# A planner's lengths and transfer model, the rank of its row maxima, and tail scores in four quadrants

## The chip, the cores and the metric

The kernel runs on one core of one Trainium2 chip. The metric is device time in microseconds (us), lower is better: the median of the runs. The engines are PE (TensorE, matmuls; its weight loads are PEld), DVE (VectorE), ACT (ScalarE), POOL (GpSimd) and SP (SyncE, which here only issues DMAs). Each engine takes its instructions in the order in which the program gives them.

## The reference

Attention over 4 batches, 8 heads, 576 positions, 64 features, then two mixture layers on the 512 joined features:

```python
q_rot, k_rot = (rotate(q), rotate(k))
scores = scale * np.matmul(q_rot, k_rot.transpose(0, 1, 3, 2))
scores = scores - np.max(scores, axis=-1, keepdims=True)
attn = np.exp(scores); attn = attn / (np.sum(attn, axis=-1, keepdims=True) + 1e-09)
x = np.matmul(attn, v)
# first mixture layer; x_prev is x one position earlier
xk = mu_k * x + (1.0 - mu_k) * x_prev
xr = mu_r * x + (1.0 - mu_r) * x_prev
k = np.maximum(xk @ w_k, 0.0); v = k * k @ w_v
x = 1.0 / (1.0 + np.exp(-(xr @ w_r))) * v
# second mixture layer
h = np.maximum(x @ w_in, 0.0); u, v = (h[..., :512], h[..., 512:])
v_n = (v - mean(v)) / np.sqrt(var(v) + 1e-06)
out = (u * (np.einsum('ts,bsd->btd', w_spatial, v_n) + b_spatial[None, :, None])) @ w_out
```

## The kernel before, in words

**The parts.** Attention of all four batches is interleaved with the first mixture layer's two large products (w_k, w_v). Both are cut into steps, and a planner written in Python puts the steps into an order for each engine. Behind it come the rest of the first layer (w_r and the gate) and the second layer, in an order written out by hand (line 785 on). Their tiles take the place of attention's, so their weight loads start once attention is over.

**Units.** Two heads make a pair, four pairs a batch. A pair's 576 rows of queries are four blocks of 128 and a tail of 64. A batch has 18 units (`which`, line 297): eight blocks of pairs 0 to 3 (units 0 to 7, first two blocks of each), two tail units (8 and 9, each with the last 64 rows of two pairs), eight more blocks. 72 units in all, eight of them tails. A unit goes through these steps, one line of the plan each (lines 538 to 558):

- `scores` (L318, PE): two PSUM tiles `s`; for a block, head j of the pair in tile j, contraction over 64 rows of the array; each tile has 288 columns in each of two halves, so 4 calls of matmul. For a tail, pair u has tile u, its two heads on the upper and lower 64 partitions: 8 calls. There are only two `s` tiles, so a unit's scores wait for the exponentials of the unit before. A call appears in the trace as two matmuls.
- `top` (L324, DVE, twice): the negated maximum of each row. `expo` (L329, ACT, twice): the exponential with its sum. `norm` (L334, L335, DVE). `high` (L341, ACT, twice) and `low` (L345, DVE, twice): the scaled probabilities as two f16 parts, into `p16`.
- `turn` (L350): SP issues one DMA that transposes `p16` into `pt`, of which there are three.
- `values` (L370, PE): 36 matmuls of 128x64 (72 for a tail), which read `pt` and `vv`; `gather` (L380 to L388, ACT) copies to `xt`, and POOL stores it (L397, L399).

**What comes ahead of a pair.** SP loads q and k (L218, L220) into one of two `raw` buffers; `rope` on DVE (L225, L226) rotates them into `rot` and so frees `raw`. v is loaded (L230), its maximum taken (L234), spread over the partitions by POOL (L238), split (L253, L258) and copied on SP (L263, L264).

**First mixture layer** (`moe1`, line 476), twice a batch, of 256 and 320 positions: `mix` (L415 to L422), dots with w_k (L432, PE) and with w_v (L462, PE), squares between them (L441 to L450), the result stored by SP (L474). The weights w_k and w_v come in 16 loads (L157) at the start, each joined from two words on ACT and DVE (L162 to L174).

**The planner** (`Plan`, line 39). Each step has a rank (about the unit in which it is due), an engine, a length in us, the steps and the buffers that it needs. `order` (line 55) runs a clock: whenever an engine is free it takes, of its next 80 steps by rank, the first whose needs are done and whose buffers are free. The program is then given out in that order, and on the chip each engine follows it, whatever the true lengths are. A step with `dma` adds to one queue of transfers (lines 81 to 83): it lands when all transfers ahead of it have had their lengths. `HOP`, 0.15, is added to each end.

Of the kernel before, what the change touches and what calls it, by code (L numbers as in the profile page):

```python
# [7 lines left out]
F32 = mybir.dt.float32  # L8
# [14 lines left out]
HALF = S // 2  # L23
# [15 lines left out]
class Plan:  # L39
# [15 lines left out]
    def order(self):  # L55
# [4 lines left out]
        while any(todo.values()):  # L60
# [7 lines left out]
            for engine, xs in todo.items():  # L68
                if free.get(engine, 0.) > now:
                    continue  # L70
                for k, x in enumerate(xs[:80]):
                    rank, _, _, us, fn, name, needs, take, use, dma = x
                    t = max([done.get(n, 1e9) for n in needs], default=0.)
                    tags = [tag for tag, _ in take]
                    if t > now:
                        soon.append(t)
                    elif all(self.room[tag] >= tags.count(tag) for tag in tags):
                        for tag in tags:
                            self.room[tag] -= 1
                        end = free[engine] = now + us  # L80
                        if dma:
                            queue = max(queue, end + 1.2) + dma
                            end = queue + .5
                        done[name] = end + self.HOP
                        back.append((end + self.HOP, [b for _, b in take] + list(use)))
                        out.append((now, x))
                        del xs[k]
                        break
# [8 lines left out]
def body(ctx: ExitStack, tc, qp, kp, vp, cs, mu_k, mu_r, w_k, w_v, w_r, w_in, w_sp, b_sp, w_out, out):  # L97
# [111 lines left out]
    def prep(i, s):  # L209
# [61 lines left out]
        for w in range(2):  # L271
# [7 lines left out]
            else:  # L279
                add(r - 2, "SP", .1, lambda w=w: load(1 - w, 0), ("ld", i, 1 - w), needs=pace(r - 2),  # L280
                    take=[("raw", ("raw", i, 1 - w))], dma=2.2)
                needs = [("ld", i, 1 - w)]
            add(r, "DVE", 2.2, lambda w=w: rope(1 - w), ("rope", i, 1 - w), needs=needs, use=[("raw", i, 1 - w)],
                take=[("rot", ("rot", i, 1 - w))])
        add(s - 5, "SP", .1, v_load, ("vl", i), needs=pace(s - 5), take=[("vr", ("vr", i))], dma=1.2)
        add(s - 3.5, "DVE", .8, v_max, ("vmax", i), needs=[("vl", i)], use=[("vr", i)], take=[("vm", ("vm", i))])
# [4 lines left out]
        add(s - .4, "DVE", .89, v_low, ("vlow", i), needs=[("v5", i)], use=[("vm", i), ("vr", i)])  # L291
        add(s - .3, "SP", .2, v_copy, ("vcopy", i), needs=[("vlow", i)], use=[("vv", i)], dma=.4)

# [13 lines left out]
    def scores(m):  # L307
        ps = [ps_s.tile([128, 2, 512], F32, tag="s", name=f"s{n}")
              for n in (2 * m, 2 * m + 1)]
        w = which(m)  # L310
        for u in range(2 if w[0][2] == 64 else 1):
            i, c, n, _ = w[u]
            q, k = preps[i][0], preps[i][1]
            for h in range(2):
                for j in range(2):
                    r = HEAD[j]
                    o = ps[u][r, h, :HALF] if n == 64 else ps[j][:, h, :HALF]
                    nc.tensor.matmul(o, q[r, c:c + n], k[r, h * HALF:(h + 1) * HALF], start=True, stop=True)  # L318
        sm = at.tile([128, 4, 2], F32, tag="sm", bufs=4, name=f"sm{m}")
        units[m] = [[x[:, :, :HALF] for x in ps], sm, [None, None], None]  # L320
# [35 lines left out]
    def values(m):  # L356
# [6 lines left out]
        for us in ((0,), (1,)) if w in (8, 9) else ((0, 1),):  # L363
            for kc in range(NKC):
                for hl in range(2):
                    for j in range(2):
                        u = us[j % len(us)]
                        i, _, n, o = which(m)[u]
                        a = pt[:, u, kc, HEAD[j]] if n == 64 else pt[:, u, kc, :]
                        nc.tensor.matmul(pv[HEAD[j], o:o + n], preps[i]["vv"][:, kc, j, D * hl:D * hl + D], a,  # L370
# [65 lines left out]
    def k_square(b, h, fc):  # L436
        ps = mo.pop((b, h, "k", fc))[:, :PART[h][1]]
        if fc % 2 == 0:
            mo[b, h, "s"] = moe_tile([128, 2, PART[1][1]], F32, "rl", 2, name=f"rl{b}_{h}_{fc}")[:, :, :PART[h][1]]
        rl = k2 = mo[b, h, "s"]  # L440
        nc.scalar.activation(rl[:, fc % 2, :], ps, AF.Relu)  # L441
# [34 lines left out]
    def moe1(b, h):  # L476

        end = UN * b + (20 if h else 10)
        s, places = end + 1.6, 16 if h else 20
        at_ = lambda m: s + .5 * (m * places / 16)  # L480
# [17 lines left out]
        for fc in range(NFC):  # L498
            m = at_(fc)
            bank, q, r = ("m", P, fc), fc // 2, ("rl", P, fc // 2)  # L500
            for k in range(2):
                add(m + .1 * k, "PE", .9 * f, lambda fc=fc, k=k: k_dot(b, h, fc, k), ("k", P, fc, k),
                    needs=[("x3", P, 2 * k), ("x3", P, 2 * k + 1)] + [("wlo", c + 4 * (fc // 4)) for c in (2 * k, 2 * k + 1)]
# [11 lines left out]
        for dc, half in ((0, 0), (1, 0), (0, 1), (1, 1), (2, 0), (2, 1), (3, 0), (3, 1)):  # L515
            m = at_(8 + n)
            n += 1
            for k in (2 * half, 2 * half + 1):
                add(m + .1 * (k % 2), "PE", .9 * f, lambda dc=dc, k=k: v_dot(b, h, dc, k), ("v", P, dc, k),
                    needs=[("kl", P, k), ("wlo", 8 + 2 * k), ("wlo", 9 + 2 * k)] + ([("v", P, dc, k - 1)] if k else []),  # L520
                    take=[] if k else [("m", ("mv", P, dc))], use=[("kk", P, k)] + ([("mv", P, dc)] if k else []))
            if half:
                add(m + .6, "ACT", .39 * f, lambda dc=dc: v_out(b, h, dc), ("vo", P, dc), needs=[("v", P, dc, 3)],
                    use=[("mv", P, dc)], take=[("mf", ("vs", P, dc))])
                add(m + 1, "SP", .1, lambda dc=dc: v_store(b, h, dc), ("vst", P, dc), needs=[("vo", P, dc)],
                    use=[("vs", P, dc)], dma=.6)
# [7 lines left out]
    for m in range(N):  # L534
        b, w = divmod(m, UN)
        pairs = sorted({u[0] for u in which(m)})
        rots = [(i, a) for i in pairs for a in range(2)]
        add(m - .5, "PE", 1.17, lambda m=m: scores(m), ("s", m), needs=[("rope", *r) for r in rots] + [("s", m - 1)][:m],
            use=[("rot", *r) for r in rots], take=[("s", ("s", m, 0)), ("s", ("s", m, 1)), ("sm", ("sm", m))])
        for j in range(2):  # L540
            add(m - .4 + .01 * j, "DVE", .71, lambda m=m, j=j: top(m, j), ("top", m, j), needs=[("s", m)], use=[("s", m, j)])
            add(m - .3 + .01 * j, "ACT", .93, lambda m=m, j=j: expo(m, j), ("exp", m, j), needs=[("top", m, j)],
# [6 lines left out]
        add(m, "DVE", .37, lambda m=m: norm(m), ("norm", m), needs=[("exp", m, 0), ("exp", m, 1)], use=[("sm", m)])  # L549
        add(m + .7, "SP", .1, lambda m=m: turn(m), ("turn", m),  # L550
            needs=[("low", m, 0), ("low", m, 1)] + [("turn", m - 1)][:m], use=[("p16", m)],
            take=[("pt", ("pt", m))], dma=3.4)
        first = w in (0, 4, 8, 10, 14)
        if first:
            bank = ("pvb", m)
        add(m + 1.5, "PE", 1.15, lambda m=m: values(m), ("pv", m),
            needs=[("turn", m)] + [("vcopy", i) for i in pairs] + ([("pv", m - 1)] if m else []),
            use=[("pt", m)] + [("vv", i) for i in pairs] + ([] if first else [bank]), take=[("pvb", bank)] if first else [])
        if w in (3, 7, 9, 13, 17):
# [5 lines left out]
            for i in mine:  # L565
# [3 lines left out]
                if w != 9:  # L569
                    add(m + 2.5, "POOL", .7, lambda i=i, h=int(w > 9): x_store(i, h), ("xst", i, w > 9),  # L570
                        needs=[("xt", m), ("edge", i)] + ([("xt", UN * b + 9)] if w > 9 else []),
                        use=[("xt", i, int(w > 9))], dma=1.2)

# [6 lines left out]
    for c in range(16):  # L580
# [6 lines left out]
        ww, wg = ("ww", c), ("wg", c)  # L587
        add(c - 2, "SP", .1, fns[0], ("wl", c), needs=pace(c - 2), take=[("kk", ww)], dma=2.)
        add(c + .2, "ACT", 1.4, fns[1], ("wsc", c), needs=[("wl", c)], use=[ww], take=[("wg", wg)])
# [264 lines left out]
```

## Time and profile before

| what | before |
|---|---|
| median of 3 runs | 818.85 us (816.68 to 818.96) |
| the profiled execution | 818.47 us, span 816.7 us |
| PE busy | 716.5 us (88%), PEld 622.7 (76%) |
| DVE busy | 548.4 us (67%) |
| ACT busy | 487.0 us (60%) |
| POOL busy | 107.8 us (13%) |
| mean granted clock of PE | 0.941 |
| DMA queue of SP (q1) | 195794 packets, 107.79 MB, 58.0% of 16 engines' span |

The span is the time from the first to the last instruction of the profiled execution; the time of a run is a little longer. Busy shares are means over parts with different limits, so a change is judged in the stretch where it lies. The profile's chain is followed back from the last instruction to whatever released it; its waits name who ended an engine's idle time. The granted clock is the share of PE's full 2.4 GHz; 0.5 is the lower level, 1.2 GHz.

### The profile page before, as it was taken

The page shows a single profiled execution, that of the slowest core. Times are in us where ns is not written, and L with a number is a line of the kernel's source. Part 1 is how long each engine was busy: PE and PEld are TensorE (multiplying, and loading weights), DVE is VectorE, ACT ScalarE, POOL GpSimd, SP SyncE. Part 2 cuts the span into 40 slices and gives each one's busy share as a digit, 9 for nine tenths or more (in the row PEclk, how much of TensorE's full clock was granted, in tenths as well). Part 3 has the DMA queues.
Part 4 walks back from the last instruction along what each step waited for, and adds up shares of the span by engine and source line. Part 5 has one row for each costly group of instructions (what it writes and reads, how often), then busy time and mean ns, then how long its engine had stood idle before and what let it go on. Part 6 is the DMA issues. An engine that isn't in the chain of part 4 may idle for free.

```text
span 816.7 us, 16914 instructions
## 1 busy us (share of the span) xinstructions
PE 716.5 (88%) x6872; PEld 622.7 (76%) x6872; DVE 548.4 (67%) x935; ACT 487.0 (60%) x980; POOL 107.8 (13%) x171
## 2 busy tenths in 40 slices
PE   2267698779999689998899997978899999999997
PEld 1144477558888568897688887977899999998997
DVE  4997999877589887689975664768756232635211
ACT  2657877569678488577695886876633412523311
POOL 0214312111001010001110001351301000201000
PEclk9975889969999889999799999998999999999999
DMA  7879987888589967699986767567210302010101
GB/s 252 248 174 192 248 198 133 201 175 147 148 192 210 209 129 160 134 210 218 180 140 126 127 126 191 164 202 243 59 59 1 117 8 96 29 31 1 59 1 59
DMA packets 197552, 114.19 MB, mean 140 GB/s; under 512 B 172961, under 2 KB 177057, under 8 KB 197474
## 3 DMA queue, kind: packets, MB, share of 16 engines
q1 hardware_dynamic: 195794, 107.79, 58.0%
q0 software_dynamic: 1536, 4.73, 1.8%
q8 instruction: 54, 0.88, 0.4%
q10 hardware_dynamic: 144, 0.59, 0.2%
q14 instruction: 24, 0.20, 0.1%
HBM read 52.26 MB, written 14.16 MB: 81 GB/s over the span
## 4 chain that ended last, share of the span: by engine, by line
PE 50%; DVE 4%; ACT 4%; DMA 4%; issue 1%; POOL 0%; DVEq 0%; ACTq 0%; SPq 0%
PE sp L625 7%; PE mv L462 6%; PE mk L432 6%; PE o L625 6%; PE s L318 5%; PE hv L699 5%; PE r L625 5%; PE u L625 5%; PE pv L370 4%; DMA pt<-p 1%; DMA I-8206_8207<-w_sp 1%; DMA I-8247_8248<-w_out 1%; DMA I-7579_7580<-w_in 1%; DMA I-7623_7624<-w_in 1%; DVE sm L324 1%
## 5 line engine op out<-in xcount | busy, mean ns | idle before, releaser
L318 PE MATMUL s<-rot,rot 64*128 64x288 f32 (+1 forms) x640 | 129.1, 481 | 55.6 <-ACT pf L329 41.9
L329 ACT ACTIVATE pf<-s,sm 128x576 f32<-128x576 f32 x144 | 106.2, 739 | 58.7 <-DVE sm L324 57.9
L318 PEld LDWEIGHTS s<-rot,rot 64*128 64x128 f32 (+1 forms) x640 | 66.9, 199 | 91.9 <-ACT pf L329 55.9
L432 PE MATMUL mk<-x,wk 128*128 128x256 f32 (+1 forms) x768 | 121.0, 307 | 12.0 <-ACT x L420 7.1
L341 ACT ACTIVATE p<-pf,sm 128x576 f16<-128x576 f32 x144 | 109.4, 771 | 36.6 <-DVE sm L335 17.5
L324 DVE TENSOR_REDUCE sm<-s 128x1 f32<-128x576 f32 x144 | 107.0, 751 | 34.9 <-PE s L318 34.6
L345 DVE SCALAR_TENSOR_TENSOR p<-pf,sm,p 128x576 f16<-128x576 f32 x144 | 118.9, 833 | 17.2 <-ACT p L341 17.1
L432 PEld LDWEIGHTS mk<-x,wk 128*128 128x128 f32 x768 | 107.3, 193 | 25.0 <-ACT x L420 7.9
L462 PE MATMUL mv<-kk,wv 128*128 128x256 f32 (+1 forms) x768 | 117.9, 302 | 1.5 <-DVE kk L450 1.5
L370 PEld LDWEIGHTS <-vv 128*64 128x64 f16 x2880 | 89.1, 122 | 36.6 <-issue 30.0
L462 PEld LDWEIGHTS mv<-kk,wv 128*128 128x128 f32 x768 | 104.8, 189 | 14.1 <-issue 10.3
L370 PE MATMUL pv<-pt,vv 128*64 128x128 f16 (+1 forms) x2880 | 100.1, 232 | 17.0 <-DMA pt<-p 16.9
L625 PE MATMUL r<-xr,wr 128*128 128x288 f32 x384 | 55.6, 302 | 2.7 <-DVE xr L629 2.1
L625 PEld LDWEIGHTS r<-xr,wr 128*128 128x128 f32 x384 | 53.6, 194 | 3.8 <-DVE xr L629 2.6
L699 PE MATMUL hv<-wi,x 128*128 128x512 f32 x192 | 48.7, 402 | 6.9 <-ACT x L628 6.7
L625 PE MATMUL sp<-ws,vn 128*128 128x288 f32 x384 | 53.9, 295 | 0.0
L625 PE MATMUL u<-x,wi 128*128 128x288 f32 x384 | 53.6, 298 | 0.0
L625 PEld LDWEIGHTS u<-x,wi 128*128 128x128 f32 x384 | 52.8, 190 | 1.0
L625 PE MATMUL o<-g,wo 128*128 128x288 f32 x384 | 53.0, 296 | 0.5 <-ACT os L755 0.5
L625 PEld LDWEIGHTS sp<-ws,vn 128*128 128x128 f32 x384 | 52.4, 188 | 0.7
L625 PEld LDWEIGHTS o<-g,wo 128*128 128x128 f32 x384 | 51.7, 188 | 1.4 <-ACT os L755 1.2
L699 PEld LDWEIGHTS hv<-wi,x 128*128 128x128 f32 x192 | 35.9, 192 | 14.7 <-ACT x L628 6.9
(293 smaller groups left out, 836.6 us busy)
## 6 DMA issues: line engine op xcount, KB each, us to landing
raw<-kp SPq DMA_DIRECT2D x15, 576.0 KB, 4.7
raw<-qp SPq DMA_DIRECT2D x15, 576.0 KB, 4.5
vr<-vp SPq DMA_DIRECT2D x16, 320.0 KB, 3.8
v<-vd SPq DMA_DIRECT2D x16, 288.0 KB, 2.9
out<-os SPq DMA_DIRECT2D x16, 288.0 KB, 2.1
vv<-vv SPq DMA_DIRECT2D x32, 128.0 KB, 3.2
x<-xd SPq DMA_DIRECT2D x12, 288.5 KB, 3.2
xd<-xt POOLq DMA_DIRECT2D x16, 160.0 KB, 4.5
```

Source lines behind the costliest of these rows:

```text
L318: nc.tensor.matmul(o, q[r, c:c + n], k[r, h * HALF:(h + 1) * HALF], start=True, stop=True)
L324: nc.vector.tensor_reduce(sm[:, 0, j:j + 1], ps[j], axis=AX.XY, op=ALU.max, negate=True)
L329: nc.scalar.activation(pf[j].rearrange("p (a b) -> p a b", a=2), ps[j], AF.Exp, bias=sm[:, 0, j:j + 1], scale=1.0, accum_out=sm[:, 1, j:j ...
L341: nc.scalar.mul(p16[:, j, 0, :], pf[j], sm[:, 3, j:j + 1])
L345: nc.vector.scalar_tensor_tensor(p16[:, j, 1, :], pf[j], sm[:, 3, j:j + 1], p16[:, j, 0, :], op0=ALU.mult, op1=ALU.subtract)
L370: nc.tensor.matmul(pv[HEAD[j], o:o + n], preps[i]["vv"][:, kc, j, D * hl:D * hl + D], a, start=kc + hl == 0, stop=kc + hl == NKC)
L432: nc.tensor.matmul(ps[:, :PART[h][1]], wk[c][fc // 4][:, w, fc % 4 * 128:fc % 4 * 128 + 128], a[:, c, :], start=m == 0, stop=m == 11)
L462: nc.tensor.matmul(ps[:, :PART[h][1]], wv[fc][:, w, dc * 128:(dc + 1) * 128], a, start=m == 0, stop=m == 23)
L625: nc.tensor.matmul(ps[:, h, :HALF], w, a[:, h * HALF:(h + 1) * HALF], start=m == 0, stop=m == n - 1)
L699: nc.tensor.matmul(ps[:, :FS], x[a][:, d, c:c + 128], wi[w][:, d, FS:], start=k == 0, stop=k == 11)
```

## The change

It changes lengths of steps in the plan and how the plan models transfers; gives the row maxima a rank one slot lower; starts the first mixture layer's dots 0.4 of a slot later; computes a tail's scores with the second pair on the other two quadrants of the array, calls alternating between pairs, and lets `values` read the halves so; and keeps the squares' tile under a key of its own for each two blocks. The cut diff:

```diff
@@ Plan.order
                         if dma:
-                            queue = max(queue, end + 1.2) + dma
-                            end = queue + .5
+                            queue = max(queue, now + 1.2) + dma
+                            end = max(queue, end + 1.5) + .4
@@ prep: loads of q and k, of v, copy of v
-                add(r - 2, "SP", .1, lambda w=w: load(1 - w, 0), ("ld", i, 1 - w), needs=pace(r - 2),
-                    take=[("raw", ("raw", i, 1 - w))], dma=2.2)
+                add(r - 2, "SP", .4, lambda w=w: load(1 - w, 0), ("ld", i, 1 - w), needs=pace(r - 2),
+                    take=[("raw", ("raw", i, 1 - w))], dma=1.9)
-        add(s - 5, "SP", .1, v_load, ("vl", i), needs=pace(s - 5), take=[("vr", ("vr", i))], dma=1.2)
+        add(s - 5, "SP", .4, v_load, ("vl", i), needs=pace(s - 5), take=[("vr", ("vr", i))], dma=1.05)
-        add(s - .3, "SP", .2, v_copy, ("vcopy", i), needs=[("vlow", i)], use=[("vv", i)], dma=.4)
+        add(s - .3, "SP", 1., v_copy, ("vcopy", i), needs=[("vlow", i)], use=[("vv", i)], dma=.5)
@@ scores
-        for u in range(2 if w[0][2] == 64 else 1):
-            i, c, n, _ = w[u]
-            q, k = preps[i][0], preps[i][1]
-            for h in range(2):
+        for h in range(2):
+            for u in range(2 if w[0][2] == 64 else 1):
+                i, c, n, _ = w[u]
+                q, k = preps[i][0], preps[i][1]
                 for j in range(2):
                     r = HEAD[j]
-                    o = ps[u][r, h, :HALF] if n == 64 else ps[j][:, h, :HALF]
+                    o = ps[u][HEAD[j ^ u], h, :HALF] if n == 64 else ps[j][:, h, :HALF]
                     nc.tensor.matmul(o, q[r, c:c + n], k[r, h * HALF:(h + 1) * HALF], start=True, stop=True)
@@ values
-                        a = pt[:, u, kc, HEAD[j]] if n == 64 else pt[:, u, kc, :]
+                        a = pt[:, u, kc, HEAD[j ^ u]] if n == 64 else pt[:, u, kc, :]
@@ k_square
-            mo[b, h, "s"] = moe_tile(
...
-        rl = k2 = mo[b, h, "s"]
+            mo[b, h, "s", fc // 2] = moe_tile(
...
+        rl = k2 = mo[b, h, "s", fc // 2]
@@ moe1
-        s, places = end + 1.6, 16 if h else 20
+        s, places = end + 2, 16 if h else 20
-                add(m + .1 * k, "PE", .9 * f, lambda fc=fc, k=k: k_dot(b, h, fc, k), ("k", P, fc, k),
+                add(m + .1 * k, "PE", .94 * f, lambda fc=fc, k=k: k_dot(b, h, fc, k), ("k", P, fc, k),
-                add(m + .1 * (k % 2), "PE", .9 * f, lambda dc=dc, k=k: v_dot(b, h, dc, k), ("v", P, dc, k),
+                add(m + .1 * (k % 2), "PE", .94 * f, lambda dc=dc, k=k: v_dot(b, h, dc, k), ("v", P, dc, k),
-                add(m + 1, "SP", .1, lambda dc=dc: v_store(b, h, dc), ("vst", P, dc), needs=[("vo", P, dc)],
+                add(m + 1, "SP", .4, lambda dc=dc: v_store(b, h, dc), ("vst", P, dc), needs=[("vo", P, dc)],
@@ units
-        add(m - .5, "PE", 1.17, lambda m=m: scores(m), ("s", m), needs=[("rope", *r) for r in rots] + [("s", m - 1)][:m],
+        add(m - .5, "PE", 1.24, lambda m=m: scores(m), ("s", m), needs=[("rope", *r) for r in rots] + [("s", m - 1)][:m],
-            add(m - .4 + .01 * j, "DVE", .71, lambda m=m, j=j: top(m, j), ("top", m, j), needs=[("s", m)], use=[("s", m, j)])
+            add(m - 1.4 + .01 * j, "DVE", .71, lambda m=m, j=j: top(m, j), ("top", m, j), needs=[("s", m)], use=[("s", m, j)])
-        add(m + .7, "SP", .1, lambda m=m: turn(m), ("turn", m),
+        add(m + .7, "SP", 2.8, lambda m=m: turn(m), ("turn", m),
             needs=[("low", m, 0), ("low", m, 1)] + [("turn", m - 1)][:m], use=[("p16", m)],
-            take=[("pt", ("pt", m))], dma=3.4)
+            take=[("pt", ("pt", m))], dma=1.7)
-        add(m + 1.5, "PE", 1.15, lambda m=m: values(m), ("pv", m),
+        add(m + 1.5, "PE", 1.2, lambda m=m: values(m), ("pv", m),
@@ stores of x, weight loads
-                    add(m + 2.5, "POOL", .7, lambda i=i, h=int(w > 9): x_store(i, h), ("xst", i, w > 9),
+                    add(m + 2.5, "POOL", .6, lambda i=i, h=int(w > 9): x_store(i, h), ("xst", i, w > 9),
-                        use=[("xt", i, int(w > 9))], dma=1.2)
+                        use=[("xt", i, int(w > 9))], dma=.6)
-        add(c - 2, "SP", .1, fns[0], ("wl", c), needs=pace(c - 2), take=[("kk", ww)], dma=2.)
+        add(c - 2, "SP", .5, fns[0], ("wl", c), needs=pace(c - 2), take=[("kk", ww)], dma=1.8)
```

## Rows read from the trace of the kernel before

**Rows 1.** Stretch, length; PE, PEld, DVE, ACT, POOL busy us (instructions); PEclk, DMA share, GB/s.

```profile
13.00:150.00 137.00, 95.56 (x973) 68.92 (x974) 125.13 (x199) 97.96 (x202) 34.33 (x38) 0.85 0.89 210
150.00:183.00 33.00, 22.29 (x213) 17.25 (x212) 26.70 (x49) 17.39 (x37) 3.36 (x7) 0.74 0.83 173
183.00:262.00 79.00, 79.00 (x983) 66.84 (x983) 60.44 (x107) 59.91 (x133) 6.17 (x17) 1.00 0.78 169
262.00:295.00 33.00, 23.61 (x263) 18.69 (x262) 27.26 (x50) 20.18 (x43) 3.31 (x6) 0.79 0.86 187
295.00:380.00 85.00, 85.00 (x1023) 71.89 (x1023) 66.96 (x119) 63.36 (x141) 7.51 (x19) 1.00 0.85 168
380.00:410.00 30.00, 25.12 (x266) 18.50 (x264) 26.45 (x51) 20.63 (x45) 3.51 (x5) 0.83 1.04 203
410.00:496.00 86.00, 85.30 (x1092) 73.31 (x1090) 58.17 (x107) 65.82 (x146) 5.77 (x16) 1.00 0.72 131
496.00:583.00 87.00, 71.99 (x508) 67.68 (x507) 62.66 (x91) 64.72 (x116) 30.29 (x29) 0.94 0.61 185
```

**Rows 2.** The chain that ended last, in order of time: start, length (us), what.

```profile
317.86 2.09 PE s L318 x16
...
332.98 1.17 PE s L318 x8
...
336.12 1.13 PE pv L370 x36
...
338.32 1.17 PE s L318 x8
...
496.12 4.59 DMA pt<-p
```

**Rows 3.** Waits (us, times, longest): start twice, then the three gaps in turn.

```profile
PE s L318 <- ACT pf L329: 34.4, 13, 8.0
...
DVE sm L324 <- PE s L318: 4.3, 7, 2.4
...
PE pv L370 <- DMA pt<-p: 6.8, 4, 2.8
...
PE pv L370 <- DMA pt<-p: 4.4, 2, 2.2
...
PE pv L370 <- DMA pt<-p: 3.5, 2, 2.2
```

**Rows 4.** SP's issues in order of time, 129 to 159 us: start, length, what.

```profile
126.92 2.81 SPq L350 DMA_TRANSPOSE pt<-p  x1
136.54 0.33 SPq L220 DMA_DIRECT2D raw<-qp  x1
...
139.90 3.35 SPq L350 DMA_TRANSPOSE pt<-p  x1
...
157.36 0.33 SPq L220 DMA_DIRECT2D raw<-qp  x1
```

**Rows 5.** DVE's instructions in order of time, 128 to 141 us.

```profile
129.60 1.54 DVE L345 SCALAR_TENSOR_TENSOR p<-pf,sm,p 128x576 f16<-128x576 f32 x2
...
134.81 1.71 DVE L226 TENSOR_TENSOR rot<-raw 128x576 f32<-128x576 f32 x1
```

**Rows 6.** Line L318 on PE in slices of 0.24 us of one tail's scores.

```profile
317.79:318.03 0.24, 0.23 (x2) 1.00 1.24 256
318.03:318.27 0.24, 0.24 (x4) 1.00 1.19 238
```

**Rows 7.** PE's instructions in order of time, about 76 us and about 165 us.

```profile
76.55 3.18 PE L318 MATMUL s<-rot,rot 64*64 64x288 f32 x16
...
165.85 2.47 PE L318 MATMUL s<-rot,rot 64*128 64x288 f32 x8
```

**Rows 8.** The transposes' line: issue time (ns, least, median, most) and time to landing.

```profile
L350 SPq DMA_TRANSPOSE pt<-p x72: 2439/3430/5774, 27.9 to 496.1; - x72
...
DMA to landing us min/median/max: 4.6/6.1/9.1
```

More of the change, by code (lines that the diff above doesn't have):

```diff
@@ L438, in k_square @@
         if fc % 2 == 0:
-            mo[b, h, "s"] = moe_tile([128, 2, PART[1][1]], F32, "rl", 2, name=f"rl{b}_{h}_{fc}")[:, :, :PART[h][1]]
-        rl = k2 = mo[b, h, "s"]
+            mo[b, h, "s", fc // 2] = moe_tile([128, 2, PART[1][1]], F32, "rl", 2, name=f"rl{b}_{h}_{fc}")[:, :, :PART[h][1]]
+        rl = k2 = mo[b, h, "s", fc // 2]
         nc.scalar.activation(rl[:, fc % 2, :], ps, AF.Relu)
```

## The prediction

> **What bounds the kernel now.** I read four views, in this order. The table of stretches comes first [rows 1]: attention with most of the first mixture layer runs to about 501 us, the rest follows. In three long stretches (183 to 262, 295 to 380, 410 to 496) PE is busy for all but 0.7 us at a granted clock of 1.00: there PE's own work is the bound. In the others PE is not full and its clock is partly at the lower level: 150 to 183 (10.7 us idle, clock 0.74), 262 to 295 (9.4 us, 0.79), 380 to 410 (4.9 us, 0.83) and the start, 13 to 150, where PE is idle for 41 us and DVE for only 11.9. These are the places where the next batch's loads and ropes come on top of the units. From 496 to 583 PE has 15 us of idle time and the chain runs through weight loads; no step there is changed.
>
> Second, the chain of waits in order of time [rows 2]: through the full stretches it is PE, instruction after instruction. A common unit's scores take 1.17 us (8 matmuls), a tail's 2.09 (16). The attention part ends with a transposing DMA, 4.59 us.
>
> Third, the waits [rows 3]: between the full stretches PE stands for transposes, 6.8, 4.4 and 3.5 us, together 14.7. In the start it stands 34.4 us for an exponential (which itself waits for a maximum on DVE), while DVE stands only 4.3 us for scores.
>
> Fourth, why transposes are late [rows 4, 5]. DVE ends unit 14's `low` at 131.1 us (129.60 plus 1.54). SP is free from 129.7, yet unit 14's transpose is issued at 139.90, 8.8 us late: ahead of it in SP's queue stands a load of q into a `raw` buffer, and that goes at 136.54, when the rope that reads the buffer ends (134.81 plus 1.71). A load of q stands there again until 157.36. DVE does `low` before the rope, so SP's order contradicts DVE's. The order comes from the plan, which has one queue of transfers with 3.4 us for a transpose (line 552). Units whose transposes land late in the plan hold the three `pt` buffers there, later transposes start late there, and loads are placed ahead of them.
>
> **The change, part by part.** The sum is made against the profiled execution: 818.47 us, of which 816.7 are the span; the median of the three runs shown is 818.85, 0.4 more.
>
> *Tails.* Eight units (two a batch) have two pairs' last 64 rows. Now 16 matmuls use two diagonal quadrants, two at a time: in slices of 0.24 us the first holds 2, each later one 4, two running out and two new [rows 6]. That is eight steps, 2.09 us in the chain. Changed, pair 1 uses the other diagonal and calls alternate between the pairs, so four matmuls could go in one step. Four steps are what a common unit has, 1.17 us [rows 2]. Ends for the new tail: 1.17 and 2.09. I take 1.17, for that row is the nearest, the same columns in two halves of the array. Gain 0.92 each. Six tails lie in full stretches and count: 5.5 us. The first two lie in the start (the very first takes 3.18 at the lower clock [rows 7]) beside a busy DVE: nothing, at most 1.9. DVE gains little: the first maximum can't start sooner, for both banks now end together, after about 1.2 us. The values read the other half of a transposed tile, with the same instructions: nothing.
>
> The Trainium skill, "TensorE: Matmul & The Clock Gate", section "The mechanism" of its Part 3, says that matmuls start and end strictly in program order. Each call here is two matmuls on one quadrant (320 calls, 640 instructions), so by that rule a second call could overlap only one of them, one call would end per 0.24 us whatever the number of quadrants, and the tails would stay as they are. The trace does not agree: the first slice already holds 2 [rows 6], where that order would give 1.
>
> *Transfers in the plan.* SP now pays for issuing (2.8 us for a transpose; the trace has a median of 3.4 [rows 8]), the queue less (1.7 in place of 3.4). In the plan a transpose alone lands 4.85 us after its start (2.8 + 1.5 + 0.4 + 0.15), before 5.35, plus 3.4 for each one queued ahead. The trace has 4.6, 6.1 and 9.1 (least, median, most) [rows 8]. So `pt` buffers return sooner in the plan, and transposes move ahead of the loads that now hold them up. No instruction is added; 72 transposes, 32 loads and the rest only change places on SP. What is late next are the ropes, whose loads come behind 3.4 us of issue; by their ranks (line 269) they have two to four units before their use. Gain: from nothing to the 14.7 us of [rows 3]. DVE is idle for 15.6 us in the same three stretches [rows 1], so DVE permits no more either. I take a third, 5 us, since part of these waits is the landing itself.
>
> *Values placed earlier.* The same edit puts `values` earlier in PE's order, where scores and dots queue behind it and the second layer's x waits for it. In the full stretches PE has a backlog and this costs nothing; elsewhere (233 of 483 us up to 496 [rows 1], so some 35 of the 72 units) each may stand up to the difference of 0.5 us between the plans: 0 to 17 us. I take 2, near the lower end, since the old order already stood only 14.7 us.
>
> *Maxima one slot earlier.* On DVE they pass ropes, weight joins, `norm` and `low` of the unit before. In the start, PE's 34.4 us for exponentials [rows 3] would shrink, but DVE is the bound there: at most its 11.9 idle us [rows 1] can come back. On the other side a maximum placed right behind its scores makes DVE stand where the scores take 2.47 us at the lower clock [rows 7] and not the plan's 1.24: a clock of 0.85, 0.74, 0.79 and 0.83 [rows 1] means the level of 1.2 GHz in place of 2.4 for 30, 52, 42 and 34% of these stretches, 82 us, some 14 units, by 1.2 us each 17. Gains reach 11.9, losses 17, neither is excluded; the waits seen so far are 4.3 us [rows 3], near the middle: zero.
>
> *First mixture layer 0.4 of a slot later.* A unit in a full stretch takes 5.34 us (332.98 to 338.32), of which 1.17 and 1.13 are scores and values [rows 2], so 3.0 are dots; 0.4 of that is 1.2 us of dots a batch, moved into stretches with idle PE, the last into 496 to 583. Up to 4.8; I take 2. The other lengths (PE's 1.24, 1.2, 0.94, POOL's 0.6, SP's stores) and the key of the squares' tile add no instruction; they act only through the order: nothing.
>
> **Sum:** 818.5 - 5.5 - 5 + 2 + 0 - 2 = 808.0 us, which I take for the median too.
>
> **The rivals.**
> - *Only the tails pay.* The gaps between full stretches stay, because DVE is busy for 80.4 of their 96 us [rows 1], and late transposes are replaced by late ropes: 818.5 - 5.5 = 813. For it: of the idle time left to DVE, a part is its own waiting for POOL and PE. Against: unit 14's 8.8 us of lateness came from SP's order alone [rows 4, 5].
> - *The quadrants don't overlap*, two matmuls that share rows of the array going one after the other: tails at 2.09, 808.0 + 5.5 = 813.5. Against it stand the values, 36 matmuls in 1.13 us [rows 2] that share all rows and use two column halves. The Trainium skill's rule of program order, named above, would give this time too.
> - *Slower: PE stands at values.* PE takes its queue in order; where the new plan lets a transpose land 0.5 us sooner, each of the 35 units outside the full stretches costs that, 17.5 us, with the tails' gain: 830.5. It decides once the added standing is over 0.16 us a unit (5.5 / 35) and the late loads stay. For it: the plan's 4.85 us lies below the median of 6.1 [rows 8]. Against: SP's 2.8 us now spaces transposes in the plan nearly as far as the trace does.
> - *Gain and loss cancel*, 816 to 821.
>
> **How the numbers follow.** Forecast 0.52; only the tails 0.18; no overlap 0.08; slower 0.17; cancelled 0.05. The predicted time is the forecast's, 808. A measurement of this kernel tells about 0.3%, 2.5 us, from no change. The first case counts as faster; of the second and third 0.18 of 0.26, for their 5 us is close to the bound; the fifth and the rest of these count as the same: 0.70, 0.13, 0.17. Low end: all eight tails (7.4), two thirds of 14.7 (9.8) and 4.8 of dots, 22 us: 796. High end 822: it takes in the first half of the slower case and leaves out its upper half and a little at the low end, some 2 in 10. The forecast's own range is 799 to 814.
>
> **What would show it.** In the chain a tail's scores: 1.2 us for 16 matmuls right, 2.1 wrong. On SP: transposes issued within about 4 us of their second `low`, no load ahead of them that stands more than 3 us. In the waits: PE for transposes under 10 us in the three gaps; above 20, the slower rival holds. In the table: DVE standing for scores in the start near 4 us, not 15. The forecast is wrong if the last transpose, now at 496.1 us, is issued later than 492.

## The result, and the profile after

The changed kernel takes 823.99 us (median of 15 runs, 816.97 to 828.27) beside 818.21 for the kernel before (15 runs, 816.18 to 819.84): a ratio of 1.0067 [1.0043, 1.0091], **slower by 5.8 us** where 10 us of gain were forecast. Its profiled execution is a long one of these, 828.27 us with a span of 826.4, so its trace shows some 4 us more loss than the median. All lines from the scores on stand one higher than before: L319 scores, L325 maxima, L346 `low`, L351 transposes, L371 values.

The table by stretch of the changed kernel, with the columns of [rows 1]:

```profile
13.00:150.00 137.00, 84.36 (x870) 61.10 (x872) 114.72 (x179) 87.74 (x183) 30.36 (x37) 0.73 0.84 201
150.00:183.00 33.00, 29.32 (x302) 23.42 (x299) 29.72 (x52) 22.63 (x49) 4.52 (x7) 0.92 0.78 169
183.00:262.00 79.00, 70.71 (x918) 60.32 (x919) 62.20 (x112) 57.93 (x126) 7.57 (x19) 0.98 0.88 181
262.00:295.00 33.00, 29.42 (x349) 24.64 (x348) 30.46 (x56) 24.45 (x55) 3.39 (x6) 1.00 0.88 194
295.00:380.00 85.00, 76.98 (x946) 66.16 (x946) 65.47 (x119) 60.91 (x135) 6.86 (x19) 0.94 0.84 165
380.00:410.00 30.00, 26.62 (x322) 21.52 (x321) 28.08 (x49) 21.73 (x47) 4.84 (x6) 1.00 1.02 205
410.00:496.00 86.00, 77.54 (x973) 65.18 (x972) 52.97 (x103) 60.96 (x135) 5.28 (x16) 0.94 0.70 124
496.00:583.00 87.00, 77.33 (x586) 73.11 (x585) 60.08 (x87) 62.32 (x117) 23.21 (x22) 0.94 0.62 189
```

Two things have changed places. The three gaps between the full stretches got better: PE ran 302, 349 and 322 matmuls in them where it ran 213, 263 and 266 [rows 1], at clocks of 0.92 and more. The three full stretches are no longer full: PE is idle for 8.3, 8.0 and 8.5 us, where it was idle for 0.7 in all, and does 261 matmuls fewer there. The start is worse too, 870 matmuls for 973, at a clock of 0.73 for 0.85. What was not done by 496 us is done after it (586 for 508).

The waits on PE name what it stood for (total us, times, longest); the rows are the wait for transposes from 13 to 150, 183 to 262, 295 to 380 and 410 to 496 us, then the start's waits for exponentials and for ropes, last the wait for transposes in the whole run, in the changed kernel and in the one before:

```profile
PE pv L371 <- DMA pt<-p: 21.2, 7, 7.9
...
PE pv L371 <- DMA pt<-p: 8.3, 6, 3.4
...
PE pv L371 <- DMA pt<-p: 8.0, 6, 3.0
...
PE pv L371 <- DMA pt<-p: 10.1, 7, 3.5
...
PE s L319 <- ACT pf L330: 20.7, 9, 9.1
...
PE s L319 <- DVE rot L226: 20.6, 3, 13.6
...
PE pv L371 <- DMA pt<-p: 55.5, 36, 7.9
...
PE pv L370 <- DMA pt<-p: 16.9, 11, 2.8
```

The idle time of the first two full stretches is the wait of `values` for transposes to the tenth; in the third the wait is 10.1 us beside 8.5 of idle time, since one of its waits begins before 410. Over the whole run this wait is 55.5 us in 36 waits; before it was 16.9 in 11, of which 14.7 in the gaps [rows 3]. The start's wait for exponentials did fall, 34.4 to 20.7, but 21.2 us of waiting for transposes took its place. The start's wait for ropes grew as well, from 13.4 to 20.6, but it is 23.7 in *t_oldxfer* below, which is fast.

Long stands were also followed by a lower clock: it was 1.00 in all three full stretches [rows 1] and is now 0.98, 0.94 and 0.94. An example from the third, on PE (start, length, what, and in brackets the idle time before it and what ended it):

```profile
429.34 1.20 PE L371 MATMUL pv<-pt,vv 128*64 128x128 f16 x36
...
436.86 2.13 PE L371 MATMUL pv<-pt,vv 128*64 128x128 f16 x36 [3.49 <-DMA pt<-p]
```

After 3.49 us of standing the granted clock from 436.8 to 441.1 us is 0.50, the lower level, and 36 matmuls take 2.13 us in place of 1.20. The three clocks mean the lower level for about 3, 10 and 10 us, so by estimate up to 12 us of PE's time went this way, beside the 24.8 of standing. It is the lesser part: in *y_early* below, which is as slow, the three clocks are 0.97 to 1.00.

Now the chain of the changed kernel: first the page's shares by engine and by line (its head), then some rows in order of time, as in [rows 2]:

```profile
PE 53%; DMA 27%; DVE 8%; ACT 6%; issue 4%; POOL 1%; SPq 0%; ACTq 0%; POOLq 0%; DVEq 0%
DMA pt<-p 22%; PE pv L371 8%; PE mk L433 7%; PE sp L626 7%; PE o L626 6%; PE s L319 6%; PE mv L463 5%; PE r L626 5%; PE hv L700 5%; PE u L626 5%; DVE sm L325 2%; DVE raw L225 1%; DVE p L346 1%; ACT p L342 1%; DMA I-8201_8202<-w_sp 1%
...
314.33 8.17 DMA pt<-p
322.54 1.99 PE pv L371 x36
...
326.36 1.13 PE s L319 x16
...
335.76 12.58 DMA pt<-p x2
...
502.98 6.21 DMA pt<-p
509.24 1.21 PE pv L371 x36
```

A chain that ran through PE now runs through transposes in the middle of the full stretches. The last transpose is issued at 503.0 and the last values start at 509.2, where they were at 496.1 [rows 2] and 500.7. From there on both need about the same: span minus start of the last values is 316.0 us before and 317.2 after.

The place at 322.54 shows how a late transpose spreads. PE's instructions there, then DVE's (read as above):

```profile
318.55 1.04 PE L463 MATMUL mv<-kk,wv 128*128 128x320 f32 x6
322.54 1.99 PE L371 MATMUL pv<-pt,vv 128*64 128x128 f16 x36 [2.95 <-DMA pt<-p]
324.46 1.90 PE L433 MATMUL mk<-x,wk 128*128 128x320 f32 x6
326.29 0.96 PE L319 MATMUL s<-rot,rot 64*64 64x288 f32 x12
```

```profile
321.40 0.81 DVE L346 SCALAR_TENSOR_TENSOR p<-pf,sm,p 128x576 f16<-128x576 f32 x1
327.53 1.42 DVE L325 TENSOR_REDUCE sm<-s 128x1 f32<-128x576 f32 x2 [5.31 <-PE s L319]
```

PE's dots end at 319.6 and the next instruction in its order is `values`, whose transpose lands at 322.5. Behind it wait dots and a later unit's scores, for which the trace shows no wait of their own, and DVE stands 5.31 us for these scores, so this unit's maxima, `low` and transpose are late in turn. DVE's standing for scores grew from 34.6 to 54.3 us in the whole run.

The transposes themselves are no slower (issue times in ns and time to landing, as in [rows 8]); SP's issues about unit 14, whose `low` ends at 143.5:

```profile
L351 SPq DMA_TRANSPOSE pt<-p x72: 2457/3247/5086, 28.2 to 503.0; - x72
...
DMA to landing us min/median/max: 4.5/5.4/8.4
```

```profile
143.58 2.72 SPq L351 DMA_TRANSPOSE pt<-p  x1
146.93 0.33 SPq L220 DMA_DIRECT2D raw<-qp  x1
```

The lateness on SP of [rows 4, 5] is gone: 8.8 us for unit 14 became 0.1, and landing is even a little quicker than the 6.1 us of [rows 8].

Last, the scores of one tail in slices of 0.24 us, with the columns of [rows 6]:

```profile
326.29:326.53 0.24, 0.24 (x4) 1.00 0.00 0
326.53:326.77 0.24, 0.24 (x8) 1.00 0.00 0
```

Four start in each slice where two did, and a tail takes 1.13 us in the chain, not 2.09.

### The profile page after: what moved, and what is told of

It reads as the page before. It is cut to its first block, busy times and chain, and to the rows that moved or that the text cites. A ratio compares the mean times of both kernels' runs of the same rounds, so it can differ in the third digit from the quotient of the medians.

```text
span 826.4 us, 16943 instructions
## 1 busy us (share of the span) xinstructions
PE 708.3 (86%) x6872; PEld 622.2 (75%) x6872; DVE 547.9 (66%) x935; ACT 483.6 (59%) x980; POOL 106.6 (13%) x171
## 3 DMA queue, kind: packets, MB, share of 16 engines
q1 hardware_dynamic: 195794, 107.79, 57.4%
## 4 chain that ended last, share of the span: by engine, by line
PE 53%; DMA 27%; DVE 8%; ACT 6%; issue 4%; POOL 1%; SPq 0%; ACTq 0%; POOLq 0%; DVEq 0%
DMA pt<-p 22%; PE pv L371 8%; PE mk L433 7%; PE sp L626 7%; PE o L626 6%; PE s L319 6%; PE mv L463 5%; PE r L626 5%; PE hv L700 5%; PE u L626 5%; DVE sm L325 2%; DVE raw L225 1%; DVE p L346 1%; ACT p L342 1%; DMA I-8201_8202<-w_sp 1%
## 5 line engine op out<-in xcount | busy, mean ns | idle before, releaser
L319 PE MATMUL s<-rot,rot 64*128 64x288 f32 (+1 forms) x640 | 114.9, 495 | 43.3 <-ACT pf L330 22.8
L371 PE MATMUL pv<-pt,vv 128*64 128x128 f16 (+1 forms) x2880 | 101.3, 233 | 55.5 <-DMA pt<-p 55.5
L371 PEld LDWEIGHTS <-vv 128*64 128x64 f16 x2880 | 91.8, 123 | 73.6 <-issue 58.8
L325 DVE TENSOR_REDUCE sm<-s 128x1 f32<-128x576 f32 x144 | 103.5, 751 | 54.6 <-PE s L319 54.3
L346 DVE SCALAR_TENSOR_TENSOR p<-pf,sm,p 128x576 f16<-128x576 f32 x144 | 117.0, 826 | 21.2 <-ACT p L342 21.2
L433 PE MATMUL mk<-x,wk 128*128 128x256 f32 (+1 forms) x768 | 124.4, 312 | 3.6 <-DVE x L423 2.1
L433 PEld LDWEIGHTS mk<-x,wk 128*128 128x128 f32 x768 | 110.0, 198 | 18.7 <-issue 10.5
L342 ACT ACTIVATE p<-pf,sm 128x576 f16<-128x576 f32 x144 | 110.5, 774 | 13.5 <-issue 4.3
L319 PEld LDWEIGHTS s<-rot,rot 64*128 64x128 f32 (+1 forms) x640 | 60.3, 203 | 72.4 <-ACT pf L330 31.6
```

The costliest lines, as they stand in the source:

```text
L325: nc.vector.tensor_reduce(sm[:, 0, j:j + 1], ps[j], axis=AX.XY, op=ALU.max, negate=True)
L342: nc.scalar.mul(p16[:, j, 0, :], pf[j], sm[:, 3, j:j + 1])
L346: nc.vector.scalar_tensor_tensor(p16[:, j, 1, :], pf[j], sm[:, 3, j:j + 1], p16[:, j, 0, :], op0=ALU.mult, op1=ALU.subtract)
L433: nc.tensor.matmul(ps[:, :PART[h][1]], wk[c][fc // 4][:, w, fc % 4 * 128:fc % 4 * 128 + 128], a[:, c, :], start=m == 0, stop=m == 11)
```

## The experiments

Medians are compared with the kernel before in runs of the same chip (818.3 to 818.7 us in each group); "before" and "after" name the two kernels. "Stands for transposes" is PE's wait of `values` in the whole run, in the profiled execution.

**One part at a time.** *t_tails* is before with the scores and values of the changed kernel and nothing else. *t_oldxfer* is after with the old plan of transfers: the formula, the lengths on SP and POOL and the transfer times; tails, rank, PE's lengths and later dots stay. *t_oldtop* is after with the old rank, *t_late* after with all landings 1.6 us later in the plan.

```diff
 t_tails, against before
-                    o = ps[u][r, h, :HALF] if n == 64 else ps[j][:, h, :HALF]
+                    o = ps[u][HEAD[j ^ u], h, :HALF] if n == 64 else ps[j][:, h, :HALF]
...
 t_oldxfer
-                            queue = max(queue, now + 1.2) + dma
-                            end = max(queue, end + 1.5) + .4
+                            queue = max(queue, end + 1.2) + dma
+                            end = queue + .5
...
-        add(m + .7, "SP", 2.8, lambda m=m: turn(m), ("turn", m),
+        add(m + .7, "SP", .1, lambda m=m: turn(m), ("turn", m),
-            take=[("pt", ("pt", m))], dma=1.7)
+            take=[("pt", ("pt", m))], dma=3.4)
 t_oldtop
-            add(m - 1.4 + .01 * j, "DVE", .71, ...
+            add(m - .4 + .01 * j, "DVE", .71, ...
 t_late
-                            end = max(queue, end + 1.5) + .4
+                            end = max(queue, end + 1.5) + 2
```

> The kernel before with nothing but the tails' scores (and the halves that values reads) changed; plan, lengths and ranks as before. If a tail's shorter scores pay where PE is the bound, 6 times 0.96 us come back: about 812.5 us, 5.8 less than before. If the order of before leaves gaps that take the gain in, 816 to 819. Waits of PE for transposes stay near 17 us in both cases.

Measured: 816.12 us, ratio 0.9977 [0.9955, 0.9999]. Tails take 1.13 us, yet only 2.2 us come back, not 5.5: in the full stretches PE does 3196 matmuls where it did 3098, but in the gaps 692 where it did 742. Its standing for transposes is 17.1 us.

> The changed kernel with the model of transfers and the lengths of SP's and POOL's issues put back to those of before; tails, rank of the maxima, PE's lengths and the dots' later start stay. Theory one (transposes land too early in the new plan, so values stand too early in PE's order): waits of PE for transposes fall from 55 us to 15 to 25, and the time to 808 to 814. Theory two (the maxima pass the low parts on DVE and make transposes late): waits stay over 45 us and the time over 821.

Measured: **801.30 us**, 0.9800 [0.9769, 0.9832], 17 us below before and 22.7 below after. Its full stretches, then its waits and landings (its profiled execution took 808.4 us):

```profile
183.00:262.00 79.00, 79.00 (x999) 67.57 (x1000) 66.58 (x118) 62.08 (x137) 6.32 (x18) 1.00 0.90 192
295.00:380.00 85.00, 84.27 (x1046) 71.51 (x1048) 72.81 (x128) 64.78 (x143) 8.04 (x18) 1.00 0.93 191
410.00:496.00 86.00, 83.45 (x1074) 72.64 (x1073) 52.45 (x96) 63.10 (x141) 7.66 (x17) 0.98 0.73 144
```

```profile
PE pv L371 <- DMA pt<-p: 9.4, 9, 2.5
...
DMA to landing us min/median/max: 4.6/5.8/10.0
```

Time and waits both fell further than theory one had them, and theory two is out. With the old plan of transfers PE is nearly full again. That transposes are late on SP does not stand against it: from the end of a unit's second `low` to the issue of its transpose, in the timelines of DVE and SP, it takes 4.15 us on average (42 units over 3 us), 2.66 in before (29 units), 2.65 in t_tails (27 units) and 0.3 in the changed kernel (none over 2.0). With 9.4 us of standing, `values` are seldom ahead of their data in PE's order, and PE does dots meanwhile.

> The changed kernel with the maxima's rank back at the unit's own slot; the new model of transfers stays. Theory one: waits of PE for transposes stay over 45 us, time 820 to 828. Theory two: waits fall to 15 to 25 us and the time to 808 to 814.

Measured: 827.25 us, 1.0101 [1.0064, 1.0137]; stands for transposes 52.5 us. The earlier rank is not the cause.

> The changed kernel whose plan lets every transfer land 1.6 us later (a transpose alone 6.45 us after its start in place of 4.85); SP's lengths and the queue stay new. Theory one: values move back in PE's order, waits of PE for transposes fall to under 30 us, time 806 to 814, and if SP's order is right besides, it is below the run with the old model. Theory two: waits over 45 us, time over 820.

Measured: 809.72 us, 0.9906 [0.9874, 0.9938]; stands for transposes 23.2 us. One number of the plan gives back 14 us. It does not come below t_oldxfer, so no gain from SP's new order shows; transposes are issued late again, 3.4 us on average.

**The parts in other company.** *x_notop* is t_oldxfer with the old rank, *x_tailtop* before with tails, rank and the key of the squares' tile, *x_turn* after with the transpose's own two numbers put back, and *x_slack* t_oldxfer with each landing 0.8 us later.

```diff
 x_notop, against t_oldxfer
-            add(m - 1.4 + .01 * j, "DVE", .71, ...
+            add(m - .4 + .01 * j, "DVE", .71, ...
 x_tailtop, against t_tails
-            add(m - .4 + .01 * j, "DVE", .71, ...
+            add(m - 1.4 + .01 * j, "DVE", .71, ...
-        rl = k2 = mo[b, h, "s"]
+        rl = k2 = mo[b, h, "s", fc // 2]
 x_turn
-        add(m + .7, "SP", 2.8, lambda m=m: turn(m), ("turn", m),
+        add(m + .7, "SP", .1, lambda m=m: turn(m), ("turn", m),
-            take=[("pt", ("pt", m))], dma=1.7)
+            take=[("pt", ("pt", m))], dma=3.4)
 x_slack, against t_oldxfer
-                            end = queue + .5
+                            end = queue + 1.3
```

> The version of 801 us (old model of transfers, all else changed) with the maxima's rank back at the unit's own slot: tails, PE's lengths and the dots' later start remain. If the rank is what brought the 15 us beyond the tails, this run is at 812 to 818, PE's waits for exponentials rise from 33 us to over 40; if PE's lengths and the later dots brought them, it stays at 800 to 806.

Measured: 810.78 us, 0.9892 [0.9864, 0.9919]. That lies between the two marks, and PE's waits for exponentials are 39.3 us. Against t_oldxfer the rank is worth 9.5 us; and the old plan of transfers gains 16.5 with the old rank too (t_oldtop's 827.25 less 810.78).

> The kernel before with the new tails and the maxima's rank alone (and the key of the squares' tile); PE's lengths and the dots' start as before. If the rank brought it: 800 to 806. If the lengths and the later dots: 812 to 818.

Measured: 810.11 us, 0.9883 [0.9859, 0.9906]. Again between the marks: against t_tails rank and key are worth 6.0 us, and lengths and dots the other 8.8 to t_oldxfer; stands for transposes 7.2 us, the least of all.

> The changed kernel with the transpose's two numbers alone put back (0.1 on SP, 3.4 in the queue); the new formula and the lengths of the other issues stay. If the slack that the plan gives transposes is the whole cause of the 22 us between the changed kernel and the one with the old model: 799 to 808, waits of PE for transposes 8 to 20 us. If the formula or the other lengths matter too: 812 to 822.

Measured: 810.12 us, 0.9888 [0.9855, 0.9922]; stands for transposes 29.0 us. Between the marks: the transpose's two numbers give back 13.9 of the 22.7 us, so they are not the whole cause. The formula and the other lengths were not tried apart.

> The version of 801 us with every transfer landing 0.8 us later in the plan. If PE's 9 us of waits for transposes there still cost time: 796 to 801. If values now come too late and hold buffers: 802 to 808.

Measured: 832.39 us, 1.0175 [1.0140, 1.0210], the slowest of all and a miss. The start lost most of all stretches, a third of the 276 matmuls that are missing by 496 us (start of t_oldxfer, then of x_slack):

```profile
13.00:150.00 137.00, 95.82 (x944) 69.84 (x946) 126.78 (x201) 94.56 (x198) 33.33 (x38) 0.81 0.88 211
```

```profile
13.00:150.00 137.00, 86.58 (x852) 62.39 (x853) 120.73 (x190) 90.15 (x187) 33.96 (x36) 0.76 0.82 197
```

PE does 92 matmuls fewer there. It stands 15.5 us for transposes in the whole run, so this is another loss than that of the changed kernel: here a plan that sees all transfers later is costly too. Which transfer does it was not isolated.

**How much an order scatters.** `HOP`, the plan's allowance of 0.15 us between engines, set to 0.14 or 0.16 means nothing in itself but changes the order on every engine. It was done to after, and to t_oldxfer (*old*).

```diff
 n_after14, n_old14 (n_after16, n_old16: .16)
-    HOP = .15
+    HOP = .14
```

> The changed kernel with 0.14 in place of 0.15 for the constant that the planner adds to every step's end: an edit without meaning, which still reorders most of the program. If the new model of transfers itself is the cause, this run too is above 818 with over 40 us of PE waiting for transposes. If orders merely scatter, it may land anywhere from 800 to 830.

> The same with 0.16. Cause in the model: above 818, over 40 us of waits for transposes. Scatter: anywhere from 800 to 830.

> The version of 801 us (old model of transfers, all else changed) with 0.14 in place of 0.15. Cause in the model: 796 to 810, under 25 us of PE waiting for transposes. Scatter: anywhere from 800 to 830.

> The same with 0.16. Cause in the model: 796 to 810, under 25 us of waits for transposes. Scatter: anywhere from 800 to 830.

Measured: after 830.96 us (1.0162 [1.0131, 1.0193]) and 818.37 (1.0005 [0.9975, 1.0035]), with 824.0 at 0.15; old 794.64 (0.9714 [0.9692, 0.9736]) and 806.65 (0.9853 [0.9798, 0.9908]), with 801.3 at 0.15. PE stands for transposes 57.4 and 51.3 us in the first two, 16.8 and 8.3 in the other two; n_old14 is a little below its mark, the others are within theirs for a cause in the model. The means of the three are 824.4 and 800.9: 23.5 us apart, with a scatter of about 6 us to each side and no overlap. The plan of transfers is therefore a cause and no accident of one order; and the 5.8 us of the changed kernel against before lie within the scatter of its own orders. The kernel before was not reordered so: how far its own 818 us are one order's luck is not known. n_old14 is the fastest version of this study, faster than both kernels.

**The landing alone, from both sides.** *y_turnlate* is after with only the transposes' landings 1.6 us later; *y_early* is t_oldxfer with a transpose's transfer halved, which lets it land after 3.65 us in the plan when nothing is queued (0.1 + 1.2 + 1.7 + 0.5 + 0.15). *n_late14* and *n_late16* are t_late with the two values of `HOP`.

```diff
 y_turnlate
-                            end = max(queue, end + 1.5) + .4
+                            end = max(queue, end + 1.5) + (2 if name[0] == "turn" else .4)
 y_early, against t_oldxfer
-            take=[("pt", ("pt", m))], dma=3.4)
+            take=[("pt", ("pt", m))], dma=1.7)
```

> The changed kernel whose plan lets the transposes alone land 1.6 us later; all other numbers of the new model stay. If the early landing of transposes is the cause: 803 to 815, PE's waits for transposes under 30 us. If the other lengths and the formula are: 818 to 830, waits over 40 us.

Measured: 810.19 us, 0.9906 [0.9876, 0.9936]. Full stretches and waits of y_turnlate:

```profile
183.00:262.00 79.00, 76.77 (x984) 66.67 (x980) 68.19 (x122) 62.70 (x141) 7.44 (x20) 0.98 0.92 196
295.00:380.00 85.00, 80.25 (x1049) 69.39 (x1049) 72.56 (x129) 62.82 (x141) 8.57 (x19) 1.00 0.94 194
410.00:496.00 86.00, 79.11 (x1056) 69.48 (x1052) 49.39 (x91) 56.64 (x129) 6.09 (x15) 0.96 0.69 139
```

```profile
PE pv L371 <- DMA pt<-p: 21.5, 15, 3.5
```

> The version of 801 us with 1.7 in place of 3.4 for a transpose in the queue, all else as there (0.1 on SP, old formula): a transpose lands 3.65 us after its start in the plan. If early landing is the cause: 818 to 830, waits of PE for transposes over 40 us. If not: 796 to 810, waits under 25 us.

Measured: 822.93 us, 1.0054 [1.0018, 1.0089], so 21.6 us lost against t_oldxfer. Full stretches and waits of y_early:

```profile
183.00:262.00 79.00, 72.07 (x919) 61.28 (x919) 58.91 (x105) 54.02 (x121) 6.64 (x18) 0.97 0.87 171
295.00:380.00 85.00, 76.16 (x981) 63.60 (x981) 71.08 (x127) 64.22 (x141) 7.59 (x19) 0.99 0.89 178
410.00:496.00 86.00, 78.31 (x1039) 66.67 (x1036) 61.02 (x117) 66.78 (x146) 5.99 (x17) 1.00 0.74 125
```

```profile
PE pv L371 <- DMA pt<-p: 71.5, 41, 9.8
```

One number of the fast version brings the whole picture of the changed kernel: transposes leave SP at once (0.19 us late on average), PE stands for them 71.5 us, and all three full stretches have holes. One number the other way mends three fifths of it in the changed kernel (13.8 of 22.7 us).

> The run with every transfer landing 1.6 us later, with 0.14 for the planner's constant. If the later landing is what helped: 800 to 816, waits under 30 us. If the 810 was scatter: about 824.

> The same with 0.16. Later landing helps: 800 to 816, waits under 30 us. Scatter: about 824.

Measured: 812.29 us (0.9917 [0.9887, 0.9947]) and 810.65 (0.9885 [0.983, 0.994]); with 809.7 the mean is 810.9, 13.5 us below the mean of after's three orders, and no order of one overlaps the other. These three lie within 2.6 us, so not every family scatters as much. PE stands for transposes 20.0 and 16.9 us.

## Why the prediction was wrong

The new plan lets a transpose land after 4.85 us when nothing is queued. The traces have medians of 5.3 to 6.2 us and longest ones of 8 to 11.4. So `values` come in PE's order ahead of their data, and PE, which takes its instructions in order, stands. The new plan of transfers cost about 23 us. Later landings of transposes alone gave back 13.8 of them (y_turnlate); earlier landings alone, put into the old plan, cost 21.6 (y_early). The rest of the change gained about 17.

- **The failed step** is "in the full stretches PE has a backlog and this costs nothing". A backlog helps an engine only if it may choose from it, and here the backlog stands *behind* the waiting `values`. The three full stretches lost 8.3, 8.0 and 8.5 us of PE's time, about as much as their waits for transposes, 26.4 us, which the sum put at nothing. Outside them, where I had counted 35 units and taken 2 us of 17, the standing grew from some 16 to 29 us. In the whole run it grew from 16.9 to 55.5 us. That this is 0.54 us for each of all 72 units, close to the 0.5 that the two plans differ by, is luck: it is made of 36 waits of 1.5 us on average, and y_early, which lands transposes 1.7 us earlier than t_oldxfer, stands 0.86 us a unit more. The slower rival thus named the right mechanism and erred on its place: its mark, over 20 us of this wait in the three gaps, did not appear (3.3, 1.9 and 1.7 us there), because the standing came in the full stretches and the start. The forecast's own mark, under 10 us there, came true (6.9) beside a wrong time: the three gaps were the wrong place to look. The rival also took the late loads to stay; they went. Its 830.5 us is too slow: the plan cost 23 us and not 17.5, but the other parts gained 17 and not 5.5.
- **Transfers on SP, -5.** The lateness went as forecast (8.8 to 0.1 us for unit 14), but it was never a price of that size. t_oldxfer has more of it than before (4.15 us a unit for 2.66) and is 17 us faster. I read SP's contradiction of DVE's order as a loss, without asking whether PE had other work placed ahead of the late `values`. It had.
- **Tails, -5.5.** Right for one tail (2.09 to 1.13, 0.96 us each), wrong for the sum: t_tails gained 2.2. The gaps took back about half of it: against 98 matmuls more in the full stretches stand 50 fewer there, where the granted clocks were 0.74, 0.71 and 0.83 for 0.74, 0.79 and 0.83. The matmuls of four quadrants run at once: four start in the first slice where the old tail had two, so the rival without overlap is out. The Trainium skill, "TensorE: Matmul & The Clock Gate", section "The mechanism", says that matmuls start and end in program order. That would keep the old tail's time only if the two matmuls of a call follow each other in PE's order. The trace does not record that order, so this run refutes the rival and not the rule; the prediction's reading of [rows 6] against the rule rests on the same assumption.
- **Maxima, 0.** Measured with others' parts held fixed: 6.0 us (t_tails to x_tailtop, with the key), 9.5 (x_notop to t_oldxfer) and 3.3 (t_oldtop to after). Single differences of this size lie near the scatter of orders, and the intervals of the third pair overlap; no pair shows a loss. The standing that I feared, DVE behind scores, is there in two of the three: in the whole run it grows by 13 us with the earlier rank, 18.1 to 31.4 (x_notop to t_oldxfer) and 40.5 to 54.3 (t_oldtop to after), and only from t_tails to x_tailtop it does not (32.3 to 30.2). It cost no time that shows. The new plan of transfers adds 22 to 23 us to it with either rank. In the start DVE stands 11.7 us in the changed kernel, not 4, and 4.3 in t_oldxfer with the same rank: what adds to it is again the plan of transfers.
- **PE's lengths and later dots, -2.** Together 5.3 us (t_tails to x_notop) and 8.8 (x_tailtop to t_oldxfer), the first with the key; the two edits were not tried apart.

From before by t_tails and x_tailtop to t_oldxfer the gains are 2.2 + 6.0 + 8.8 = 17.0 us. The mark set for a wrong forecast, a last transpose later than 492 us, came true at 503.0.

What stays open: why landings 0.8 us later cost t_oldxfer 31 us, while 1.6 us later helped the changed kernel; what of the formula and the other lengths makes the 9 us that the transposes' landing leaves; and with a scatter of about 6 us for one order, the parts under that, and the 17 us against a kernel before of one order, are signs more than sizes.

## What to carry to other kernels

Where a plan fixes the order of an engine that takes its work in turn, a transfer that the plan lands too early can cost that engine's time even where it has a backlog, since the backlog stands behind the wait; a late issue on a queue cost nothing that showed here, where other work was placed ahead of its user. Landing everything later is no safe way out: it gave 14 us in one kernel and cost 31 in the other. So before a length of the plan is set to a least or middle value of the trace, ask which engine waits if the transfer takes its usual or its longest time. Before a small difference between two planned orders is believed, reorder each with an edit that means nothing and compare the families: here the scatter was about 6 us to each side, and the best order of the better family was 24 us faster than the kernel before.

## What was not expected of the hardware

Four matmuls on four quadrants of 64 x 64 start within 20 ns (326.293, 326.300, 326.307 and 326.313 us), though the program gives its calls one after the other, and a tail of 16 takes 1.13 us, no more than the 1.17 of a common unit's 8 matmuls [rows 2]. A wait of 3.49 us on PE was followed by 36 matmuls at the lower clock, 2.13 us in place of 1.20. A transpose of the same size lands after 4.5 to 11.4 us in these runs, while the median of a run only moves from 5.3 to 6.2.
